# One float32 matmul of 512 columns for two of 256 in the last product of a fused attention and two-MLP kernel

## The chip, the cores and the metric

The kernel runs as one program on one core of one Trainium2 chip. The metric is the time of the whole program on the device in microseconds (us). Engines are named as the profile names them: PE is TensorE (its matmuls), PEld its weight loads, DVE VectorE, ACT ScalarE, POOL GpSimd, SP the engine that issues most transfers.

## The reference, cut to what matters

Causal attention over 4 batches of 8 heads gives `x` of 2304 tokens and 512 features; a first MLP with a normalisation follows, then the second MLP, whose last line the change is about:

```python
def _moe2_ref(x, w_in, w_out):          # x: 2304 x 512, w_in: 512 x 2048, w_out: 2048 x 512
    h = x @ w_in
    relu6 = np.clip(h + 3.0, 0.0, 6.0)
    g = h * relu6 / 6.0
    return (g @ w_out).astype(np.float32)
```

All is float32.

## The kernel before

**Order of the work.** The kernel writes no engine's program by hand. Each piece of work is told to a planner (class `Plan`) with its engine, a duration, what it reads and writes, and buffers or PSUM banks that it takes. `Plan.emit` plays these pieces through with the given durations, lets each engine take the ready piece of lowest rank, and emits the instructions in the order in which they came up; the engines then run their lists strictly in that order. A piece's rank is its running number, changed for some ranges of numbers by the table `MOVED` (line 46), which holds plain running numbers (for instance `(3517, 3518, None, -22)`); the table is the same in both kernels.

**The stages.** Attention comes first, with the first MLP laid between; then the second MLP's first product (`unit`, line 1367), which writes `g` to HBM in transposed form; from 594 us to the end runs the second MLP's second product, `g @ w_out / 6`. It is the stage that the change touches.

**The second product.** The tokens are cut into 9 tiles (`group(bi, t)`, line 1493; 3 `bi` by 3 `t`) of 256 tokens by 512 output columns. Such a tile is computed as a 2 x 2 block product by the scheme with seven products and fifteen sums: `a11, a12, s2, s1, s3, s4, a22` (table `SECOND`, line 1443), each of a 128-token block by a 256-column block of weights, over 8 slices of 128 of the inner dimension. Three accumulators live in PSUM banks, `x`, `y` and `z`: `x` takes `a11`, then `s2`, `s3` and `a22` on top, `y` takes `a12`, `z` takes `s1`, then `s4`.

**High and low.** A float32 factor is split into a rounded high part and the rest, the low part. `form` (line 1525) makes both parts of a token block: ACT casts the high part (line 1533), then DVE, or POOL for two forms of each tile from the third tile on, subtracts to get the low part (line 1537). Four form buffers go round. Before that, DVE makes the sums of the scheme, `n`, `r21`, `r11` and `r12` (`total`, line 1517), each of 128 x 1024. The weights are split beforehand and lie side by side: `W[:, k, 0, :]` is the high and `W[:, k, 1, :]` the low part of 256 columns.

**The matmuls.** `product` (line 1548) issues, for each slice k, high x W high and high x W low (`y = 0`, one piece per two or three slices), then low x W high (`y = 1`), each a matmul of 256 columns into the first 256 columns of the accumulator's bank: 24 matmuls a product, 168 a tile, 1512 in all.

**Reading the banks.** `x` is read in the middle of its accumulation, so that PE may not go on with it until it is read. `keep` (line 1562) copies `x / 6` to SBUF on ACT: `c11` after `a11`, `c12` after `s2`, `c22` after `s3`. `put` (line 1569) makes an output block: on DVE as `bank / 6 + kept` (`y` with `c11`, `z` with `c22` after `s1`, `z` with `c12` after `s4`), on ACT for the last one (`x` after `a22`); SP then stores it. Line 1587 lists these tails.

The planner gives a DVE operation on two SBUF tensors and any POOL operation the same single port (`port`), so that it never plans them side by side.

Of the kernel before, what the change touches and what calls it, by code (L numbers as in the profile page):

```python
# [16 lines left out]
ALU = mybir.AluOpType  # L17
# [187 lines left out]
def act(n, extra=0.09):  # L205
    return extra + 0.00085 * n
# [11 lines left out]
def kernel(ctx, tc, q, k, v, s, w_in, w_out, g_ln, w2_in, w2_out, out):  # L218
    nc = tc.nc
# [4 lines left out]
    P = 128  # L224
# [58 lines left out]
    def bank(key):  # L283
        return banks[plan.bank[key]]
# [147 lines left out]
    NK = KFF2 // 2  # L432
    T = {}
# [107 lines left out]
    plan = Plan()  # L541
# [951 lines left out]
    def group(bi, t):  # L1493


        tag = f"{bi}_{t}"
        nonlocal slots
        mine = slots
        slots = dict(r11=mine["n"], r12=mine["r21"], r21=mine["r11"], r22=mine["r12"], n=mine["r22"])
        key = lambda x: f"{x}_{tag}"  # L1500
        made, done = [], []

        def raw_tile(x):
            i = mine[x]
# [36 lines left out]
        made.append([load("r21", 1, 0), load("r22", 1, 1)] + form("a12", "r12", "DVE"))
        made.append([total("n", "r21", "r22", 1), total("r21", "r11", "r21", 0), total("r11", "n", "r11", 0)] + form("s2", "r11", "DVE"))
        made.append(form("s1", "n", "POOL" if forms_made[0] > 14 else "DVE"))
        made.append(form("s3", "r21", "DVE"))
        made.append([total("r12", "r12", "r11", 0)] + form("s4", "r12", "DVE"))
        made.append(form("a22", "r22", "POOL" if forms_made[0] > 14 else "DVE"))

        def product(x, i, b, first):
            b_key, name = key(f"o{b}"), key(f"f{x}")
            r = []  # L1550
            for y in range(2):
                for q, (k0, k1) in enumerate(PIECES):
                    def mm(y=y, q=q, k0=k0, k1=k1):
                        for k in range(k0, k1):
                            for w in range(2 - y):
                                nc.tensor.matmul(bank(b_key)[:, : 2 * P], lhsT=T[name][:, y, k, :], rhs=T[f"W{i}_{q}"][:, k - k0, w, :],  # L1556
                                                 start=first and k == 0 and y == 0 and w == 0, stop=k == NK - 1 and y == 1, skip_group_check=not first)

                    r.append(lambda mm=mm, y=y, q=q, n=k1 - k0: plan.add("PE", n * (2 - y) * 0.119, mm, reads=[f"{name}/{'hl'[y]}", *(f"W{i}_{q}/{w}" for w in "hl"[: 2 - y])], writes=[b_key], bank=b_key if first and y == q == 0 else None))
            return r  # L1560

        def keep(name, b):
            def go():
                T[key(name)] = pools["mid"].tile([P, W], F32, tag=name, name=key(name), bufs=2)[:, : 2 * P]
                nc.scalar.mul(T[key(name)], bank(key(f"o{b}"))[:, : 2 * P], 1.0 / 6.0)

            return [lambda: plan.add("ACT", act(2 * P), go, reads=[key(f"o{b}")], writes=[key(name)], new=[(name, 2, key(name))])]

        def put(b, h, o, kept):
            ob = key(f"ob{h}{o}")  # L1570

            def go():
                T[ob] = pools["g"].tile([P, W], F32, tag="g", name=ob, bufs=G_BUFS)[:, : 2 * P]
                src = bank(key(f"o{b}"))[:, : 2 * P]
                if kept:
                    nc.vector.scalar_tensor_tensor(out=T[ob], in0=src, scalar=1.0 / 6.0, in1=T[key(kept)], op0=ALU.mult, op1=ALU.add)
                else:
                    nc.scalar.mul(T[ob], src, 1.0 / 6.0)

            def store():  # L1580
                r0 = ((2 * bi + h) * TRIO + t) * P
                nc.sync.dma_start(out=out[r0 : r0 + P, o * 2 * P : (o + 1) * 2 * P], in_=T[ob])

            return [lambda: plan.add(*(("DVE", dve(2 * P)) if kept else ("ACT", act(2 * P))), go, reads=[key(f"o{b}")] + ([key(kept)] if kept else []), writes=[ob], new=[("g", G_BUFS, ob)]),
                    lambda: plan.add("SP", 0.5, store, reads=[ob], writes=[f"out{ob}"], dma=moved(128, 1024))]

        tails = [keep("c11", "x"), put("y", 0, 0, "c11"), keep("c12", "x"), [], keep("c22", "x") + put("z", 1, 1, "c22"), put("z", 0, 1, "c12"), put("x", 1, 0, None)]
        for (x, i, b, first), tail in zip(SECOND, tails):
            done.append(product(x, i, b, first) + tail)
        return made, done  # L1590
# [80 lines left out]
```

## Time and profile before

| | |
|---|---|
| median of 3 runs | 784.19 us (782.44 to 785.3) |
| the profiled execution | 783.54 us, of which its span from first to last instruction is 781.7 us |
| granted TensorE clock, mean | 0.998 of full speed |
| PE busy | 766.9 us, 98% of the span |
| DVE, ACT, POOL busy | 600.4, 476.8, 229.0 us |
| chain of waits that ended last | PE 91%, DVE 3%, ACT 2%, DMA 2%; the second product's matmuls (line 1556) 22% |

The profile is one execution. An engine's busy time counts instructions that overlap only once, and a matmul's listed duration runs from its start to the modelled end of its write, so that a stream of matmuls is read by the distance between starts. The chain of waits is followed back from the last instruction. Below, a "cast" is ACT's high part, a "low" the subtraction that makes the low part.

### The profile page before, as it was taken

To read this page: it belongs to the slowest core of one execution; us is meant where nothing else is said; L and a number is where in the kernel's file an instruction comes from. 1 tells how busy PE (TensorE), PEld (TensorE's weight loads), DVE (VectorE), ACT (ScalarE), POOL (GpSimd) and SP (SyncE) were. 2 spreads that over 40 slices of the span, in tenths; PEclk is the share of its full clock that TensorE was granted. 3 is DMA by queue.
4 is the path that set the end of the run, shared out by engine and by line. 5 is a ranking of instruction groups with operands and counts; after the bars stand their busy time and mean duration, and the time that the engine had idled before them with its cause. 6 is when DMAs were issued, how large, how long until landed. Compare 5 with 4: busy or idle time off the path is not lost.

```text
span 781.7 us, 15872 instructions
## 1 busy us (share of the span) xinstructions
PE 766.9 (98%) x5560; PEld 705.5 (90%) x5560; DVE 600.4 (77%) x1381; ACT 476.8 (61%) x1071; POOL 229.0 (29%) x320
## 2 busy tenths in 40 slices
PE   6999999999999999999999999999999999999998
PEld 5667878988898888888999999999999999999998
DVE  5789988677967787757787897898987877766663
ACT  4889878656767566646474765666675444444332
POOL 3584635344643363252200000000122012222222
PEclk9999999999999999999999999999999999999999
DMA  8867677788577685613533544567599644444440
GB/s 203 207 175 205 167 184 200 200 212 203 142 191 191 185 193 151 182 54 136 157 106 91 197 164 174 184 214 267 157 293 417 199 134 135 137 135 135 136 135 28
DMA packets 157615, 136.33 MB, mean 174 GB/s; under 512 B 67616, under 2 KB 135200, under 8 KB 157536
## 3 DMA queue, kind: packets, MB, share of 16 engines
q1 hardware_dynamic: 153600, 122.07, 55.1%
q10 hardware_dynamic: 2400, 8.54, 3.4%
q0 software_dynamic: 1536, 4.72, 1.5%
q8 instruction: 44, 0.72, 0.4%
q14 instruction: 35, 0.29, 0.1%
HBM read 74.67 MB, written 39.39 MB: 146 GB/s over the span
## 4 chain that ended last, share of the span: by engine, by line
PE 91%; DVE 3%; ACT 2%; DMA 2%; issue 1%; SPq 0%; ACTq 0%; DVEq 0%
PE bank L1556 22%; PE bank L1379 22%; PE bank L1129 13%; PE bank L1039 12%; PE bank L934 6%; PE bank L839 5%; PE bank L907 5%; PE bank L1108 2%; PE bank L688 1%; PE bank L803 1%; DMA s_sb<-in_s_dram 1%; DMA raw_wi<-in_moe_w_in_dram 1%; DMA V0b<-in_v_dram 0%; ACT y L760 0%; DVE y L748 0%
## 5 line engine op out<-in xcount | busy, mean ns | idle before, releaser
L1379 PE MATMUL bank<-xb,ws 128*128 128x384 f32 x1008 | 176.6, 336 | 0.0
L1379 PEld LDWEIGHTS bank<-xb,ws 128*128 128x128 f32 x1008 | 175.3, 188 | 0.0
L1556 PE MATMUL bank<-W,fs 128*128 128x256 f32 x864 | 106.3, 282 | 0.2 <-ACT fs L1533 0.2
L1556 PEld LDWEIGHTS bank<-W,fs 128*128 128x128 f32 x864 | 104.3, 190 | 0.4 <-ACT fs L1533 0.4
L855 POOL TENSOR_SCALAR y<-y,rsum 128x256 f32<-128x256 f32 (+4 forms) x120 | 72.1, 618 | 103.4 <-DVE rsum L851 65.3
L760 ACT ACTIVATE y<-y,nmax 128x384 f32<-128x384 f32 (+4 forms) x140 | 83.4, 598 | 19.9 <-DVE nmax L748 18.0
L748 DVE CUSTOM_DVE_ANT_0 y<-bank,mask 96x288 f32<-96x288 f32 (+4 forms) x168 | 73.5, 466 | 22.1 <-PE bank L839 17.1
L1129 PE MATMUL bank<-zh,w_out_h 128*128 128x256 f32 x288 | 82.3, 286 | 0.0
L1556 PE MATMUL bank<-W,fa 128*128 128x256 f32 x648 | 81.0, 282 | 0.2 <-ACT fa L1533 0.2
L1129 PE MATMUL bank<-zh,w_out_l 128*128 128x256 f32 x288 | 81.0, 281 | 0.0
L1129 PE MATMUL bank<-zl,w_out_h 128*128 128x256 f32 x288 | 80.9, 281 | 0.0
L1556 PEld LDWEIGHTS bank<-W,fa 128*128 128x128 f32 x648 | 78.9, 190 | 0.4 <-ACT fa L1533 0.4
L1413 POOL DMA_DIRECT2D g_d<-g x24 | 13.2, 552 | 184.9 <-DVE g L1408 184.9
L1039 PE MATMUL bank<-w_in_h,xh 128*128 128x512 f32 x144 | 59.6, 414 | 0.1
L839 PE MATMUL bank<-stack 128*96 128x288 f32 (+4 forms) x288 | 58.8, 321 | 0.0
L1039 PE MATMUL bank<-w_in_h,xl 128*128 128x512 f32 x144 | 56.5, 393 | 0.0
L1039 PE MATMUL bank<-w_in_l,xh 128*128 128x512 f32 x144 | 56.5, 392 | 0.0
L1129 PEld LDWEIGHTS bank<-zh,w_out_h 128*128 128x128 f32 x288 | 54.2, 188 | 1.3 <-issue 0.2
L1129 PEld LDWEIGHTS bank<-zh,w_out_l 128*128 128x128 f32 x288 | 54.2, 188 | 0.5
L1392 ACT COPY c<-bank 128x384 f32<-128x384 f32 x72 | 34.2, 478 | 33.3 <-PE bank L1379 31.3
L1129 PEld LDWEIGHTS bank<-zl,w_out_h 128*128 128x128 f32 x288 | 54.3, 188 | 0.0
L907 PE MATMUL bank<-ident,y 128*128 128x128 f32 (+2 forms) x420 | 50.8, 260 | 1.0 <-POOL y L873 0.7
(275 smaller groups left out, 1575.1 us busy)
## 6 DMA issues: line engine op xcount, KB each, us to landing
r<-g_d SPq DMA_DIRECT2D x36, 512.0 KB, 5.8
g_d<-g SPq DMA_DIRECT2D x72, 192.0 KB, 1.9
rawo<-in_moe_w_out_dram SPq DMA_DIRECT2D x16, 512.0 KB, 4.7
rawi<-in_moe_w_in_dram SPq DMA_DIRECT2D x16, 512.0 KB, 5.1
x_d<-x2s SPq DMA_DIRECT2D x36, 128.0 KB, 2.5
xr<-x_d SPq DMA_DIRECT2D x6, 768.0 KB
g_d<-g POOLq DMA_DIRECT2D x24, 192.0 KB, 5.9
W<-wp_d SPq DMA_DIRECT2D x6, 768.0 KB, 10.5
```

The lines of the kernel that those rows point to most:

```text
L748: nc.vector.tensor_tensor_reduce(out=ys[h, t][:n, c0:c1], in0=bank(key)[:n, : c1 - c0], in1=mask[:n, 480 + n - w + c0 : 480 + n - w + c1], ...
L760: nc.scalar.activation(out=y[:n], in_=y[:n], func=AF.Exp, bias=nmax[:n, h, t : t + 1], scale=-1.0, accum_out=sums[:n, h, t : t + 1])
L839: nc.tensor.matmul(bank(key)[:n, : c1 - c0], lhsT=ss[:, 2 - 2 * m, ST[t] : w], rhs=ss[:, 3 - 2 * m, c0:c1], start=(m == 0), stop=(m == 1))
L855: nc.gpsimd.tensor_scalar(ys[h, t][:n], ys[h, t][:n], rsum[:n, h, t : t + 1], 1.0, ALU.mult, ALU.mult)
L907: nc.tensor.transpose(bank(key)[: SZ[jj], c : c + SZ[t]], ys[h, t][: SZ[t], ST[jj] : ST[jj] + SZ[jj]], ident[: SZ[t], : SZ[t]])
L934: nc.tensor.matmul(bank(key)[j * D : (j + 1) * D, lo - c0 : c1 - c0], lhsT=vs[v_key(p, a)][:n, jj, j, :], rhs=pts[pt_key(2 * p + j, a)][:n ...
L1039: nc.tensor.matmul(bank(key), lhsT=xs[i][m // 2][:, kk, :], rhs=(w_in_l if m == 1 else w_in_h)[:, kk, f * 512 : (f + 1) * 512], start=(kk ...
L1108: nc.tensor.transpose(bank(key)[:, m * P : (m + 1) * P], es[i][:, f, m * P : (m + 1) * P], ident)
L1129: nc.tensor.matmul(bank(key)[:, : 2 * P], lhsT=w_out_at(w, kk)[:, m * P : (m + 1) * P], rhs=z[:, kk, :], start=(kk == 0 and i == 0), stop= ...
L1379: nc.tensor.matmul(bank(key)[:, :W], lhsT=T[f"ws{k}"][:, WS_OF[op], a, kc * P : (kc + 1) * P], rhs=x_form(bi, op)[:, b, kc, :], start=(fir ...
L1392: nc.scalar.copy(T[to], bank(key)[:, :W])
L1556: nc.tensor.matmul(bank(b_key)[:, : 2 * P], lhsT=T[name][:, y, k, :], rhs=T[f"W{i}_{q}"][:, k - k0, w, :], start=first and k == 0 and y == ...
```

## The change

High x W high and high x W low of a slice become one matmul of 512 columns over the whole bank: the first 256 columns collect high x W high and, as before, low x W high; the second 256 collect high x W low. A product has 8 matmuls of 512 columns and 8 of 256 in place of 24 of 256. Each of the seven readings of a bank in a tile gets a second one on DVE, which adds the second half divided by 6 to what the first wrote (`rest`). A product that goes on in a bank now waits for both readings, and so does a store.

```diff
                         for k in range(k0, k1):
-                            for w in range(2 - y):
-                                nc.tensor.matmul(bank(b_key)[:, : 2 * P], lhsT=T[name][:, y, k, :], rhs=T[f"W{i}_{q}"][:, k - k0, w, :],
-                                                 start=first and k == 0 and y == 0 and w == 0, stop=k == NK - 1 and y == 1, skip_group_check=not first)
-
-                    r.append(lambda mm=mm, y=y, q=q, n=k1 - k0: plan.add("PE", n * (2 - y) * 0.119, mm, ...
+                            w = T[f"W{i}_{q}"][:, k - k0]
+                            to, by = (bank(b_key), w.rearrange("p w n -> p (w n)")) if y == 0 else (bank(b_key)[:, : 2 * P], w[:, 0, :])
+                            nc.tensor.matmul(to, lhsT=T[name][:, y, k, :], rhs=by, start=first and k == 0 and y == 0, stop=k == NK - 1 and y == 1, skip_group_check=True)
+
+                    r.append(lambda mm=mm, y=y, q=q, n=k1 - k0: plan.add("PE", n * (0.119 if y else 0.23), mm, ...
...
         def keep(name, b):
...
-            return [lambda: plan.add("ACT", act(2 * P), go, reads=[key(f"o{b}")], writes=[key(name)], new=[(name, 2, key(name))])]
+            def rest():
+                nc.vector.scalar_tensor_tensor(out=T[key(name)], in0=bank(key(f"o{b}"))[:, 2 * P :], scalar=1.0 / 6.0, in1=T[key(name)], op0=ALU.mult, op1=ALU.add)
+
+            return [lambda: plan.add("ACT", act(2 * P), go, reads=[key(f"o{b}")], writes=[f"{key(name)}/a"], new=[(name, 2, key(name))]),
+                    lambda: plan.add("DVE", dve(2 * P), rest, reads=[key(f"o{b}"), f"{key(name)}/a"], writes=[f"{key(name)}/b"])]
...
         def put(b, h, o, kept):
...
+            def rest():
+                nc.vector.scalar_tensor_tensor(out=T[ob], in0=bank(key(f"o{b}"))[:, 2 * P :], scalar=1.0 / 6.0, in1=T[ob], op0=ALU.mult, op1=ALU.add)
...
+                    lambda: plan.add("DVE", dve(2 * P), rest, reads=[key(f"o{b}"), f"{ob}/a"], writes=[f"{ob}/b"]),
+                    lambda: plan.add("SP", 0.5, store, reads=[f"{ob}/a", f"{ob}/b"], writes=[f"out{ob}"], dma=moved(128, 1024))]
```

The 63 new pieces shift the running numbers of all later ones, and the new readings and durations go into the plan, so that the order changes too. Three places follow; a name such as `fs1_0_0` is the form of `s1` in tile `0_0`, `W3_0` a third of a weight block, `bank3_98` a PSUM bank, `c12` and `ob` what `keep` and `put` write. In the new kernel `product`'s matmul stands in line 1557, `keep`'s `rest` in line 1568, `put` and its `rest` in 1580 and 1585.

PE in the first tile, before. Here bank 3 is `x`, bank 4 is `y` and bank 0 is `z`; the high matmuls of `a12` stand just ahead, those of `s3` (into bank 3) just behind.

```order
L1556 MATMUL bank0_95<-W3_0_7229,fs1_0_0_7409 128x256 x6
L1556 MATMUL bank0_95<-W3_1_7244,fs1_0_0_7409 128x256 x6
L1556 MATMUL bank0_95<-W3_2_7349,fs1_0_0_7409 128x256 x4
L1556 MATMUL bank3_98<-W6_0_7149,fs2_0_0_7433 128x256 x6
L1556 MATMUL bank3_98<-W6_1_7103,fs2_0_0_7433 128x256 x6
L1556 MATMUL bank3_98<-W6_2_7138,fs2_0_0_7433 128x256 x4
L1556 MATMUL bank3_98<-W6_0_7149,fs2_0_0_7433 128x256 x3
L1556 MATMUL bank3_98<-W6_1_7103,fs2_0_0_7433 128x256 x3
L1556 MATMUL bank3_98<-W6_2_7138,fs2_0_0_7433 128x256 x2
L1556 MATMUL bank4_99<-W1_0_7004,fa12_0_0_7394 128x256 x3
L1556 MATMUL bank4_99<-W1_1_7049,fa12_0_0_7394 128x256 x3
L1556 MATMUL bank4_99<-W1_2_7066,fa12_0_0_7394 128x256 x2
```

PE at the same place now; the high matmuls of `a12` and `s1` stand just ahead, those of `s3` into bank 3 directly behind.

```order
L1557 MATMUL bank0_95<-W3_0_7229,fs1_0_0_7398 128x256 x3
L1557 MATMUL bank0_95<-W3_1_7244,fs1_0_0_7398 128x256 x3
L1557 MATMUL bank0_95<-W3_2_7345,fs1_0_0_7398 128x256 x2
L1557 MATMUL bank4_99<-W1_0_7004,fa12_0_0_7386 128x256 x3
L1557 MATMUL bank4_99<-W1_1_7049,fa12_0_0_7386 128x256 x3
L1557 MATMUL bank4_99<-W1_2_7066,fa12_0_0_7386 128x256 x2
L1557 MATMUL bank3_98<-W6_0_7149,fs2_0_0_7417 128x512 x3
L1557 MATMUL bank3_98<-W6_1_7103,fs2_0_0_7417 128x512 x3
L1557 MATMUL bank3_98<-W6_2_7138,fs2_0_0_7417 128x512 x2
L1557 MATMUL bank3_98<-W6_0_7149,fs2_0_0_7417 128x256 x3
L1557 MATMUL bank3_98<-W6_1_7103,fs2_0_0_7417 128x256 x3
L1557 MATMUL bank3_98<-W6_2_7138,fs2_0_0_7417 128x256 x2
```

`s1`'s low matmuls and `a12`'s have moved ahead of `s2`, and between `s2` and `s3`, both on bank 3, nothing is left.

DVE in the first tile, before:

```order
L1537 TENSOR_TENSOR fs1_0_0_7409<-n_0_0_7396,fs1_0_0_7409 128x1024
L1537 TENSOR_TENSOR fs2_0_0_7433<-r11_0_0_7059,fs2_0_0_7433 128x1024
L1537 TENSOR_TENSOR fa12_0_0_7394<-r12_0_0_7124,fa12_0_0_7394 128x1024
L1537 TENSOR_TENSOR fs3_0_0_7424<-r21_0_0_7158,fs3_0_0_7424 128x1024
L1521 TENSOR_TENSOR r12_0_0_7124<-r12_0_0_7124,r11_0_0_7059 128x1024
L1576 SCALAR_TENSOR_TENSOR ob00_0_0_7503<-bank4_99,c11_0_0_7398 128x256
L1537 TENSOR_TENSOR fa22_0_0_7484<-r22_0_0_7186,fa22_0_0_7484 128x1024
L1537 TENSOR_TENSOR fs4_0_0_7505<-r12_0_0_7124,fs4_0_0_7505 128x1024
L1576 SCALAR_TENSOR_TENSOR ob11_0_0_7542<-bank0_95,c22_0_0_7526 128x256
```

and now:

```order
L1537 TENSOR_TENSOR fs1_0_0_7398<-n_0_0_7388,fs1_0_0_7398 128x1024
L1537 TENSOR_TENSOR fs2_0_0_7417<-r11_0_0_7059,fs2_0_0_7417 128x1024
L1537 TENSOR_TENSOR fa12_0_0_7386<-r12_0_0_7124,fa12_0_0_7386 128x1024
L1568 SCALAR_TENSOR_TENSOR c11_0_0_7390<-bank3_98,c11_0_0_7390 128x256
L1537 TENSOR_TENSOR fs3_0_0_7408<-r21_0_0_7158,fs3_0_0_7408 128x1024
L1580 SCALAR_TENSOR_TENSOR ob00_0_0_7448<-bank4_99,c11_0_0_7390 128x256
L1585 SCALAR_TENSOR_TENSOR ob00_0_0_7448<-bank4_99,ob00_0_0_7448 128x256
L1521 TENSOR_TENSOR r12_0_0_7124<-r12_0_0_7124,r11_0_0_7059 128x1024
L1537 TENSOR_TENSOR fs4_0_0_7466<-r12_0_0_7124,fs4_0_0_7466 128x1024
L1568 SCALAR_TENSOR_TENSOR c12_0_0_7472<-bank3_98,c12_0_0_7472 128x256
```

The reading of `c11`'s second half comes ahead of `s3`'s low; that of `c12` comes behind the sum `r12` and `s4`'s low, the two others of `ob00` ahead of `r12`.

PE in the last tile, before, from the end of `s3` (bank 3 is `x`) to the start of `a22`:

```order
L1556 MATMUL bank3_98<-W4_2_7267,fs3_2_2_9187 128x256 x2
L1556 MATMUL bank0_95<-W3_2_7349,fs1_2_2_9161 128x256 x4
L1556 MATMUL bank0_95<-W3_0_7229,fs1_2_2_9161 128x256 x3
L1556 MATMUL bank0_95<-W3_1_7244,fs1_2_2_9161 128x256 x3
L1556 MATMUL bank0_95<-W3_2_7349,fs1_2_2_9161 128x256 x2
L1556 MATMUL bank3_98<-W5_0_7317,fa22_2_2_9241 128x256 x6
```

and now:

```order
L1557 MATMUL bank3_98<-W4_0_7207,fs3_2_2_8783 128x256 x3
L1557 MATMUL bank3_98<-W4_1_7231,fs3_2_2_8783 128x256 x3
L1557 MATMUL bank3_98<-W4_2_7267,fs3_2_2_8783 128x256 x2
L1557 MATMUL bank3_98<-W5_0_7317,fa22_2_2_8824 128x512 x3
L1557 MATMUL bank3_98<-W5_1_7355,fa22_2_2_8824 128x512 x3
L1557 MATMUL bank0_95<-W2_0_7286,fs4_2_2_8798 128x512 x3
```

`a22` follows `s3` on the same bank directly; the rest of `s1`, which stood between them, has gone ahead of `s3`.

## Rows read from the trace of the kernel before

**Rows 1.** The page's first part: busy us of each engine, share of the span, instructions.

```profile
PE 766.9 (98%) x5560; PEld 705.5 (90%) x5560; DVE 600.4 (77%) x1381; ACT 476.8 (61%) x1071; POOL 229.0 (29%) x320
```

**Rows 2.** Windows: stretch, us; PE, PEld, DVE, ACT, POOL busy; PE clock, DMA share, GB/s.

```profile
604.00:614.00 10.00, 9.84 (x83) 9.64 (x82) 9.03 (x11) 4.55 (x7) 0.54 (x1) 1.00 0.97 338
...
720.00:740.00 20.00, 20.00 (x170) 20.00 (x170) 13.22 (x13) 8.24 (x12) 4.82 (x2) 1.00 0.43 132
```

**Rows 3.** Groups from 590 us on, shapes apart: count, busy us, mean ns | idle before, releaser.

```profile
L1556 PE MATMUL bank<-W,fs 128*128 128x256 f32 x864 | 106.3, 282 | 0.2 <-ACT fs L1533 0.2
```

**Rows 4.** Timelines, ACT and PE, seventh tile: start, duration (us), instruction, [idle before <-releaser].

```profile
719.89 0.38 ACT L1578 ACTIVATE ob<-bank 128x256 f32<-128x256 f32 x1 [5.79 <-PE bank L1556]
...
732.58 1.59 PE L1556 MATMUL bank<-W,fa 128*128 128x256 f32 x12
...
732.78 0.38 ACT L1565 ACTIVATE c<-bank 128x256 f32<-128x256 f32 x1 [1.74 <-PE bank L1556]
...
739.89 0.38 ACT L1578 ACTIVATE ob<-bank 128x256 f32<-128x256 f32 x1 [5.79 <-PE bank L1556]
```

**Rows 5.** Timeline of PE in the first MLP: twelve 512-column matmuls in a row, first and last.

```profile
388.16 0.39 PE L1039 MATMUL bank<-w_in_h,xh 128*128 128x512 f32 x1
...
390.66 0.39 PE L1039 MATMUL bank<-w_in_h,xl 128*128 128x512 f32 x1
```

**Rows 6.** Timeline of DVE in the seventh tile.

```profile
725.85 0.41 DVE L1576 SCALAR_TENSOR_TENSOR ob<-bank,c 128x256 f32<-128x256 f32 x1
726.18 1.21 DVE L1537 TENSOR_TENSOR fs<-r,fs 128x1024 fp32r<-128x1024 f32 x1
...
733.20 0.42 DVE L1576 SCALAR_TENSOR_TENSOR ob<-bank,c 128x256 f32<-128x256 f32 x1 [0.90 <-ACT c L1565]
```

**Rows 7.** Timeline of PE in the first tile.

```profile
600.46 2.18 PE L1556 MATMUL bank<-W,fa 128*128 128x256 f32 x16 [0.19 <-ACT fa L1533]
602.47 2.07 PE L1556 MATMUL bank<-W,fs 128*128 128x256 f32 x16
604.70 3.13 PE L1556 MATMUL bank<-W,fs 128*128 128x256 f32 x24 [0.16 <-ACT fs L1533]
...
612.42 1.58 PE L1556 MATMUL bank<-W,fa 128*128 128x256 f32 x12
```

**Rows 8.** Timeline of DVE in the first tile.

```profile
599.83 1.22 DVE L1521 TENSOR_TENSOR n<-r,r 128x1024 f32<-128x1024 f32 x1
601.08 1.23 DVE L1521 TENSOR_TENSOR r<-r,r 128x1024 f32<-128x1024 f32 x1
...
603.95 1.22 DVE L1537 TENSOR_TENSOR fs<-n,fs 128x1024 fp32r<-128x1024 f32 x1
605.09 1.22 DVE L1537 TENSOR_TENSOR fs<-r,fs 128x1024 fp32r<-128x1024 f32 x1
606.22 1.22 DVE L1537 TENSOR_TENSOR fa<-r,fa 128x1024 fp32r<-128x1024 f32 x1
607.36 1.22 DVE L1537 TENSOR_TENSOR fs<-r,fs 128x1024 fp32r<-128x1024 f32 x1
```

**Rows 9.** Timeline of ACT in the first tile: the cast of `a12`, and that of `s4`.

```profile
599.36 1.05 ACT L1533 CAST fa<-r 128x1024 fp32r<-128x1024 f32 x1 [0.55 <-DMA W<-wp_d]
...
609.80 1.05 ACT L1533 CAST fs<-r 128x1024 fp32r<-128x1024 f32 x1 [0.55 <-DVE r L1521]
```

**Rows 10.** Timeline of POOL in the seventh tile: one low.

```profile
728.47 2.41 POOL L1537 TENSOR_TENSOR fa<-r,fa 128x1024 fp32r<-128x1024 f32 x1 [4.77 <-ACT fa L1533]
```

**Rows 11.** Timelines of POOL and DVE in the fourth tile, where their subtractions meet.

```profile
661.13 1.22 DVE L1521 TENSOR_TENSOR r<-r,r 128x1024 f32<-128x1024 f32 x1
...
661.29 3.33 POOL L1537 TENSOR_TENSOR fs<-n,fs 128x1024 fp32r<-128x1024 f32 x1 [8.98 <-PE bank L1556]
...
662.27 4.58 DVE L1537 TENSOR_TENSOR fs<-r,fs 128x1024 fp32r<-128x1024 f32 x2
```

**Rows 12.** One line's view, DVE on a bank and SBUF: ns min/median/max, first and last start.

```profile
L1115 DVE TENSOR_TENSOR zl<-bank,zh x36: 676/682/693, 82.5 to 414.1; 128x512 fp32r<-128x512 f32 x36
```

More of the change, by code (lines that the diff above doesn't have):

```diff
@@ L1554, in mm @@
                         for k in range(k0, k1):
-                            for w in range(2 - y):
-                                nc.tensor.matmul(bank(b_key)[:, : 2 * P], lhsT=T[name][:, y, k, :], rhs=T[f"W{i}_{q}"][:, k - k0, w, :],
-                                                 start=first and k == 0 and y == 0 and w == 0, stop=k == NK - 1 and y == 1, skip_group_check=not first)
-                    r.append(lambda mm=mm, y=y, q=q, n=k1 - k0: plan.add("PE", n * (2 - y) * 0.119, mm, reads=[f"{name}/{'hl'[y]}", *(f"W{i}_{q}/{w}" for w in "hl"[: 2 - y])], writes=[b_key], bank=b_key if first and y == q == 0 else None))
+                            w = T[f"W{i}_{q}"][:, k - k0]
+                            to, by = (bank(b_key), w.rearrange("p w n -> p (w n)")) if y == 0 else (bank(b_key)[:, : 2 * P], w[:, 0, :])
+                            nc.tensor.matmul(to, lhsT=T[name][:, y, k, :], rhs=by, start=first and k == 0 and y == 0, stop=k == NK - 1 and y == 1, skip_group_check=True)
+                    r.append(lambda mm=mm, y=y, q=q, n=k1 - k0: plan.add("PE", n * (0.119 if y else 0.23), mm, reads=[f"{name}/{'hl'[y]}", *(f"W{i}_{q}/{w}" for w in "hl"[: 2 - y])], writes=[b_key], bank=b_key if first and y == q == 0 else None))
             return r
@@ L1582, in store @@
                 nc.sync.dma_start(out=out[r0 : r0 + P, o * 2 * P : (o + 1) * 2 * P], in_=T[ob])
-            return [lambda: plan.add(*(("DVE", dve(2 * P)) if kept else ("ACT", act(2 * P))), go, reads=[key(f"o{b}")] + ([key(kept)] if kept else []), writes=[ob], new=[("g", G_BUFS, ob)]),
-                    lambda: plan.add("SP", 0.5, store, reads=[ob], writes=[f"out{ob}"], dma=moved(128, 1024))]
+            return [lambda: plan.add(*(("DVE", dve(2 * P)) if kept else ("ACT", act(2 * P))), go, reads=[key(f"o{b}")] + ([f"{key(kept)}/{x}" for x in "ab"] if kept else []), writes=[f"{ob}/a"], new=[("g", G_BUFS, ob)]),
+                    lambda: plan.add("DVE", dve(2 * P), rest, reads=[key(f"o{b}"), f"{ob}/a"], writes=[f"{ob}/b"]),
+                    lambda: plan.add("SP", 0.5, store, reads=[f"{ob}/a", f"{ob}/b"], writes=[f"out{ob}"], dma=moved(128, 1024))]
         tails = [keep("c11", "x"), put("y", 0, 0, "c11"), keep("c12", "x"), [], keep("c22", "x") + put("z", 1, 1, "c22"), put("z", 0, 1, "c12"), put("x", 1, 0, None)]
```

## The prediction, made before the change was run

> **What bounds the kernel now.** I read the page's busy times first: PE has 98% of the span [rows 1]. The windows tell more: in a late tile of the second product PE is busy for 20.00 of 20.00 us at a granted clock of 1.00 and DVE for 13.22; in the first tile DVE has 9.03 of 10.00 us, ACT 4.55 and the DMA engines are full [rows 2]. The groups of instructions show 0.2 us of idle time ahead of 864 of the stage's 1512 matmuls [rows 3]. So after the first tile PE waits for nothing, and what shortens its stream shortens the program until another engine comes late; in the first tile DVE is the one that can. The timelines give the paces from which the sums are made.
>
> **The stream.** A tile repeats after 20.00 us (719.89 to 739.89 [rows 4]); with 168 matmuls that is 119.05 ns for one of 256 columns. Twelve matmuls of 512 columns start over 2.50 us [rows 5], eleven steps of 227.3 ns. Two of 256 take 238.1 ns, so a pair saves 10.8 ns, a product (8 pairs) 0.086 us, the 504 pairs 5.44 us. A product now lasts 8 x 0.2273 + 8 x 0.119 = 2.77 us. This very matmul the trace doesn't show; its bounds are 238.1 ns (nothing saved) and 213.3 ns, 512 columns at 2.4 GHz (24.8 ns saved, 12.5 us in all). I take 227.3, the row of the same width in a stream as dense.
>
> The Trainium skill ("TensorE: Matmul & The Clock Gate", section Back-to-back issue gap) speaks against the change: it gives a gap of columns / 2.4 GHz plus 2.5 ns, hence 109.2 and 215.8 ns, and by these, an estimate, the pair saves 2.6 ns and the stage 1.3 us. Both rows lie some 10 ns above it, so here the trace and not the rule sizes the term.
>
> **The new readings.** There are 63 on DVE. `put`'s like operation takes 0.42 us, and the next instruction starts 0.33 after it (725.85, 726.18 [rows 6]); a second one on the same output waits for the first, which I put at 0.45 from start to start, since dependent sums start 1.25 apart and independent ones 1.14 [rows 8]. Seven in a tile are 2.4 us of DVE, on 13.2 of now 19.4 us: the idle time covers them, and without it each would cost its 0.34. Not covered is what stands between a product and the next one in the same bank. PE's stream of `s3` ends at 732.58, ACT starts 0.20 later [rows 4], DVE 0.42 after ACT's start (733.20 [rows 6]), the reading takes 0.42, and a waiting PE starts 0.05 after what it waits for (cast 599.36 + 1.05, PE 600.46 [rows 7, 9]). PE can go on 1.09 us after its product, 0.45 later than now, and later still when DVE has something ahead of the reading. After a stop it loses 0.11 more (16 matmuls are 1.90, but from 600.46 the next ones start 2.01 later [rows 7]).
>
> **The first tile.** DVE's list up to the low of `a12` is as before, so its times hold: low of `s1` ready at 603.95 + 1.22 = 605.17, of `a12` at 606.22 + 1.22 = 607.44 [rows 8]. PE, by the order shown with the change:
> - high of `a12` from 600.46 (a wait for the cast, which swallows what `a11` saves), 1.82 + 0.11, then high of `s1`: done at 604.21.
> - low of `s1` waits for 605.22: 1.01 idle; done at 606.28.
> - low of `a12` waits for 607.49: 1.21 idle; done at 608.55. Before, `s2` filled this time.
> - `s2` to 611.32.
> - `s3` goes into the bank of `s2`, so `c12` must be read twice. DVE: reading of `c11` at 607.36, low of `s3` 607.70, the two readings of `y` 608.84 and 609.29, `r12` 609.63 to 610.85; ACT casts `s4` (1.05 us; it starts about 0.05 after `r12` [rows 9]) to 611.94; DVE makes its low from 611.97 and only then reads `c12`, 613.11 to 613.53. `s3` starts at 613.58: 2.26 idle.
>
> With 0.11 for each of the three stops, these four products are done at 616.46. Before, it was 612.42, when `a22` starts [rows 7]. So the first tile loses **4.04** net. As bounds for its waits I keep 0 (4.39 better) and, should each low that PE waits for come one subtraction later, 3.4 more.
>
> **The second tile.** DVE starts it with the same list, now a subtraction behind; carried on with the same steps, `c12` is read until 633.90, and PE could have started `s3` at 633.08: 0.87 + 0.11 = **0.98**.
>
> **The other tiles.** From the third on POOL makes two lows. Counted from the end of a tile's `s3`: the second reading of `c22` ends at 1.04, those of `z` at 1.94; PE comes to `s4` at 2.50 (eight high matmuls of the next `a11`, three of `a22`). DVE then runs the low of `a12` (1.86), `n` (3.00), `r21` (4.25), `r11` (5.50), `z` twice (6.64, 7.09), `r12` (7.43), the low of `s2` (8.57), and reads `ob` (9.71) and `c11` (10.05 to 10.47); PE wants that bank at 11.09. Margins of 0.5 and 0.6 us: no wait, by a little.
>
> **The last tile.** `a22` follows `s3` in the same bank with nothing between: 1.09 + 0.11 = **1.20**. The last output has one more reading after ACT's: **0.45**.
>
> **The sum.** The 58 products that follow the first tile's four and `a11` save 58 x 0.0864 = 5.01 us. 4.04 + 0.98 + 1.20 + 0.45 - 5.01 = **+1.7 us**. On the profiled execution's 783.54 that is 785.2, on the median of 784.19 785.9; I say **785.5**. A measurement of this kernel can tell about 0.5% (3.9 us) from no change.
>
> **Rivals.**
> - *The gain arrives.* The first tiles' waits are not real, because the planner would have placed PE's pieces so that they are ready: 1.7 - 4.39 - 0.98 = -3.7 us, 779.8; a little more where the 512 columns come nearer to 213 ns. For it: before, PE lost 0.33 us there in the same game (602.47 + 1.90 = 604.37, start at 604.70 [rows 7]). Against it: DVE's times up to 607.44 are read, not guessed. 0.12.
> - *POOL takes the port first: slower.* Where POOL's low comes while a DVE subtraction runs, the next DVE subtraction waits for the whole of it: POOL asks at 661.29, DVE's sum ends at 662.35, and the following low, begun at 662.27, is through with its successor only 4.58 us later, in place of 2.36 [rows 11]. In each of the seven later tiles the low of `s2` starts at 8.57 and POOL's low of `s1` is ready at 9.11 by the same count (cast of `s2` from 6.76, ACT's last reading, cast of `s1`, some 2.35 us). If DVE is later than POOL by a hair, POOL's 2.41 us [rows 10] stand ahead of the low of `s2` and of the reading of `c11` behind it; that ends at about 13.4 in place of 10.47, and PE stops 2.4 us in seven tiles: 16.8 + 1.7, 802. It decides from 0.54 us of lateness on. Against it: that margin; and the readings themselves, one operand of which is in PSUM, hardly wait (such an operation never took over 693 ns in 36, beside a POOL that was often busy [rows 12]). 0.10. The Trainium skill ("SBUF — State Buffer", section SBUF: two separate sides) says that whichever of the two starts first holds the pair of ports for its whole instruction, on DVE's side for operations with two inputs in SBUF; by it the subtractions would wait here and the readings not. The trace's 4.58 us agrees on the first.
> - *The pair costs what two did.* Writing the whole bank takes 238 ns: the 5.01 fall away, 790.2. The rows of the same width speak against it [rows 5]. 0.04. By the gap that the Trainium skill's page on TensorE, named above, gives, an estimate, 3.8 us of them fall away: 789.0.
> - *The margins of 0.5 are too thin.* Five handovers in a row, each 0.1 to 0.2 longer than read, cost up to 0.5 in seven tiles: 787 to 789. 0.08.
>
> **How the numbers follow.** Forecast 0.66 (no change), gain 0.12 (half of it beyond 0.5%), port 0.10 and pair 0.04 slower, margins 0.08, half of it slower. Faster 0.06, same 0.76, slower 0.18. The range leaves out the port and the lower half of the gain (0.16): 779.8 up to 791, which holds the pair and the margins.
>
> **What would show it.** Right: 512-column matmuls at about 227 ns, 256 still at 119; stops of PE between 604 and 614 us of some 1.0, 1.2 and 2.3 us, behind lows and behind `c12`'s second reading, one of nearly 1 us in the second tile and one of 1.1 near the end; a tile of 19.4 us between. Wrong: a steady tile of 20 us or more, PE waiting for DVE's `c11` in each, or no idle time in the first tile.

## The result, and the profile after

The changed kernel takes 788.25 us (median of 8 executions, 786.46 to 789.08) against 783.89 for the kernel before: ratio 1.0054, 95% interval 1.0038 to 1.0071. The forecast was 785.5 in a range of 779.8 to 791.0, with no measurable change as the likeliest outcome; it came out at the edge of what can be told, half a per cent slower. The second set further down gives 787.13 and 1.0035 (1.0021 to 1.0049).

The profiled execution took 788.91 us, its span 787.1. Its page answers to [rows 1], the windows to [rows 2], the groups to [rows 3]. The page:

```profile
PE 766.2 (97%) x5056; PEld 681.1 (87%) x5056; DVE 621.2 (79%) x1444; ACT 475.4 (60%) x1071; POOL 230.2 (29%) x320
```

PE has 504 matmuls fewer and as much busy time as before; DVE has 63 instructions and 21 us more. The windows (duration, then busy time and instructions of PE, PEld, DVE, ACT and POOL; granted clock of TensorE, DMA share, GB/s):

```profile
604.00:614.00 10.00, 6.19 (x37) 4.93 (x35) 8.78 (x12) 3.55 (x5) 0.54 (x1) 1.00 0.88 308
614.00:624.00 10.00, 9.80 (x43) 8.22 (x44) 5.95 (x8) 2.04 (x3) 0.00 (x0) 0.83 0.36 109
720.00:740.00 20.00, 20.00 (x116) 17.49 (x115) 16.22 (x20) 8.23 (x11) 5.26 (x2) 1.00 0.44 132
```

In the first tile PE fell from 9.84 to 6.19 of 10 us, and over the ten us behind it the granted clock had a mean of 0.83. In a late tile PE is as full as before. What PE waited for in the stage (total us, times, the longest):

```profile
PE bank L1557 <- DVE c L1568: 3.8, 3, 2.1
PE bank L1557 <- DVE fa L1537: 1.1, 1, 1.1
PE bank L1557 <- DVE fs L1537: 0.8, 1, 0.8
```

L1568 is the new second reading of a kept bank: it holds PE three times. The lows of `s1` and `a12` hold it once each. PE's timeline (start, length, instructions; in brackets the idle time ahead and what ended it) shows where; it answers to [rows 4, 7]:

```profile
601.01 2.12 PE L1557 MATMUL bank<-W,fa 128*128 128x512 f32 x8 [0.20 <-ACT fa L1533]
...
605.78 1.22 PE L1557 MATMUL bank<-W,fs 128*128 128x256 f32 x8 [0.81 <-DVE fs L1537]
608.05 1.21 PE L1557 MATMUL bank<-W,fa 128*128 128x256 f32 x8 [1.05 <-DVE fa L1537]
609.10 2.95 PE L1557 MATMUL bank<-W,fs 128*128 128x512 f32 x16
614.20 4.62 PE L1557 MATMUL bank<-W,fs 128*128 128x512 f32 x16 [2.14 <-DVE c L1568]
618.65 2.69 PE L1557 MATMUL bank<-W,fa 128*128 128x512 f32 x11
...
636.27 3.07 PE L1557 MATMUL bank<-W,fs 128*128 128x512 f32 x16 [0.70 <-DVE c L1568]
...
658.78 2.69 PE L1557 MATMUL bank<-W,fa 128*128 128x512 f32 x11
...
678.38 2.69 PE L1557 MATMUL bank<-W,fa 128*128 128x512 f32 x11
...
777.48 1.67 PE L1557 MATMUL bank<-W,fa 128*128 128x512 f32 x6 [0.93 <-DVE c L1568]
```

Three stops in the first tile (0.81, 1.05, 2.14), one in the second (0.70), one in the last (0.93). The rows 614.20 and 636.27 are the same 16 matmuls of `s3`, once 4.62 and once 3.07 us long. Between the stops a tile repeats after 19.60 us (658.78 to 678.38), 0.40 less than before. The chain of waits (start, length, what) gives the way to the 2.14:

```profile
606.86 1.13 DVE fa L1537
608.00 0.34 DVE c L1568
608.33 1.13 DVE fs L1537
609.46 0.35 DVE ob L1580
...
609.83 0.43 DVE ob L1585
610.26 1.14 DVE r L1521
...
611.50 1.06 ACT fs L1533
...
612.58 0.32 DVE fs L1537
...
613.72 0.43 DVE c L1568
...
614.20 15.82 PE bank L1557 x80
```

It is DVE's queue in the order of the prediction: low of `a12`, reading of `c11`, low of `s3`, two of `y`, `r12`, ACT's cast of `s4`, its low, and only then the reading of `c12` on which `s3` waits.

### The profile page after: what moved, and what is told of

Its sections match the earlier page's. It is cut to its first block, busy times and chain, and to the rows that moved or that the text cites. A ratio compares the mean times of both kernels' runs of the same rounds, so it can differ in the third digit from the quotient of the medians.

```text
span 787.1 us, 14967 instructions
## 1 busy us (share of the span) xinstructions
PE 766.2 (97%) x5056; PEld 681.1 (87%) x5056; DVE 621.2 (79%) x1444; ACT 475.4 (60%) x1071; POOL 230.2 (29%) x320
## 5 line engine op out<-in xcount | busy, mean ns | idle before, releaser
L1557 PE MATMUL bank<-W,fs 128*128 128x256 f32 (+1 forms) x576 | 106.4, 341 | 3.6 <-DVE c L1568 2.8
L1557 PEld LDWEIGHTS bank<-W,fs 128*128 128x128 f32 x576 | 91.6, 191 | 18.3 <-DVE c L1568 3.2
L1557 PE MATMUL bank<-W,fa 128*128 128x512 f32 (+1 forms) x432 | 79.4, 338 | 2.2 <-DVE fa L1537 1.1
L1557 PEld LDWEIGHTS bank<-W,fa 128*128 128x128 f32 x432 | 66.4, 189 | 11.0 <-DVE fa L1537 1.3
L1533 ACT CAST fs<-r 128x1024 fp32r<-128x1024 f32 x27 | 28.3, 1050 | 55.3 <-DVE r L1521 42.4
```

Source lines behind the costliest of these rows:

```text
L1557: nc.tensor.matmul(to, lhsT=T[name][:, y, k, :], rhs=by, start=first and k == 0 and y == 0, stop=k == NK - 1 and y == 1, skip_group_check= ...
```

## The experiments

**How the runs are compared.** The executions of one kernel spread over 2 to 6 us, and much of it arises ahead of the changed stage: in these profiles the stage begins between 597.5 and 603.5 us (the latest, of e4, has a granted clock of 0.89 in its first 60 us, the kernel before 0.97). So beside the medians I use the **stage**: from the start of `a12`'s high matmuls (the row at 601.01 above; 600.46 in [rows 7]) to the end of the span, in one profile of each kernel.

| kernel | median us | ratio to before, 95% | stage us |
|---|---|---|---|
| before | 782.94 to 783.89 in four sets | | 181.24 |
| changed | 788.25 | 1.0054 (1.0038 to 1.0071) | 186.09 |
| e1 split again | 789.25 | 1.0068 (1.0047 to 1.0089) | 187.58 |
| e2 no second reading | 781.72 | 0.9976 (0.9964 to 0.9988) | 181.08 |
| e3 table moved | 785.17 | 1.0025 (1.0010 to 1.0040) | 183.86 |
| e4 two tiles narrow | 781.94 | 0.9974 (0.9960 to 0.9988) | 180.32 |
| e5 old order | 781.65 | 0.9980 (0.9967 to 0.9993) | 180.76 |
| e6 reading ahead of `s4` | 785.14 | 1.0035 (1.0021 to 1.0049) | 184.57 |
| e7 three tiles narrow | 780.51 | 0.9966 (0.9953 to 0.9978) | 179.26 |
| e8 old form, new order | 786.88 | 1.0048 (1.0034 to 1.0062) | 184.42 |
| e9 one reading earlier | 784.36 | 1.0005 (0.9992 to 1.0017) | 182.62 |
| e10 first and last narrow | 782.67 | 0.9989 (0.9975 to 1.0002) | 181.55 |
| e11 changed again | 787.13 | 1.0035 (1.0021 to 1.0049) | 186.05 |

The theory is the prediction's, with its sizes corrected by the profile after: the stream saves a little, the stops eat it. Its main rivals: the wide matmul brings nothing here; the table's shifted numbers are the cause; the readings' load on DVE is. Line numbers differ by a few between the kernels.

**e1, the stream alone.** The wide matmul is cut in two, all else stays:

```diff
-to, by = (bank(b_key), w.rearrange("p w n -> p (w n)")) if y == 0 else (bank(b_key)[:, : 2 * P], w[:, 0, :])
-nc.tensor.matmul(to, lhsT=T[name][:, y, k, :], rhs=by, start=first and k == 0 and y == 0, ...)
+for x in range(2 - y):
+    nc.tensor.matmul(bank(b_key)[:, x * 2 * P : (x + 1) * 2 * P], lhsT=T[name][:, y, k, :], rhs=w[:, x, :],
+                     start=first and k == 0 and y == 0 and x == 0, ...)
```

> Each 512-column matmul is cut again into two of 256 into the two halves of the bank; halves, readings, waits and the planned order stay those of the changed kernel's form. Theory (the wide stream saves some 0.057 us a product, the readings and their waits cost the rest): the 63 products take 63 x 0.057 = 3.6 us more than in the changed kernel, the stops of the first, second and last tile stay, so some 3.6 us above the changed kernel, 7 to 8 us above the kernel before (about 791.5). Rival (the wide matmul streams no faster than the pair here, and the whole difference lies elsewhere): as the changed kernel, 4 us above the kernel before. Forecast's size of the saving (0.0864 a product): 5.4 us above the changed kernel, about 793.5.

Measured: 1.0 us above the changed kernel by the medians, with overlapping intervals; 1.5 by the stage. Expected were 3.6. PE's timeline of e1:

```profile
602.98 1.22 PE L1557 MATMUL bank<-W,fs 128*128 128x256 f32 x8 [0.68 <-DVE fs L1537]
605.25 1.22 PE L1557 MATMUL bank<-W,fa 128*128 128x256 f32 x8 [1.05 <-DVE fa L1537]
...
611.39 3.10 PE L1557 MATMUL bank<-W,fs 128*128 128x256 f32 x24 [2.04 <-DVE c L1569]
...
640.47 6.12 PE L1557 MATMUL bank<-W,fa 128*128 128x256 f32 x50
...
660.47 6.12 PE L1557 MATMUL bank<-W,fa 128*128 128x256 f32 x50
```

The stops are there, the tile is back at 20.00 us (640.47 to 660.47). So the wide matmul is worth 0.40 us a tile. The stage says less because `s3` behind the third stop takes 2.95 us here (611.39 to 614.34, the next row) and 4.45 in the changed kernel: that is the clock, below. Without those 1.5 us the stages differ by 3.0, and the stops of e1 are 0.5 us shorter in all (0.68, 2.04 and, in the second tile, 0.42 in place of 0.81, 2.14 and 0.70): together 3.5, where nine tiles of 0.40 make 3.6. The medians alone would not have told it.

**e2, the readings.** All 63 are left out (the edit in short):

```diff
-lambda: plan.add("DVE", dve(2 * P), rest, reads=[key(f"o{b}"), f"{key(name)}/a"], writes=[f"{key(name)}/b"])]
+]
...
-lambda: plan.add("DVE", dve(2 * P), rest, reads=[key(f"o{b}"), f"{ob}/a"], writes=[f"{ob}/b"]),
```

> The second reading of every bank (63 instructions on VectorE) is left out, so the product of the high part with the low part of W is computed and not added. Theory (readings make the waits): no stop of over 0.5 us behind a reading is left, and what remains is the stream's saving, 63 x 0.057 = 3.6 us below the kernel before, about 780.3; the granted clock stays at 1.00 between 614 and 624. Rival (the faster stream alone outruns the low forms of the first tile, and the readings are not to blame): stops of 0.8 and 1.0 us stay in the first tile and the gain is 1 us or less. With the forecast's pitch of 227.3 ns it would be 5.4 us below, 778.5.

Measured: 1.9 us below before instead of the 3.6 expected. No stop of DVE's making is left, but the planner, whose input this changes, made another order, and four waits for ACT came with it; the largest in PE's timeline:

```profile
644.64 8.63 PE L1553 MATMUL bank<-W,fs 128*128 128x512 f32 x48 [1.59 <-ACT fs L1529]
```

With 0.50 and 0.39 in the first tile and 0.24 in the last they are 2.72 us; the stage, 181.08, would be 178.4 without them, 2.9 below before. The forecast's saving of 5.4 doesn't come even without the readings.

**e3, the table.** The order table speaks of instructions by number, and the new readings shift the numbers behind them:

```diff
-(3467, 3487, "DVE", -24), ... (4113, 4128, None, -127), ... (3517, 3518, None, -22), ... (3559, 3564, None, 9), ... (3518, 3541, None, -65),
+(3467, 3488, 'DVE', -24), ... (4172, 4189, None, -139), ... (3520, 3521, None, -23), ... (3566, 3572, None, 10), ... (3521, 3547, None, -68),
```

> The changed kernel with the order table's plain numbers carried along past the new instructions, so that each entry hits the piece that it hit in the kernel before. The order of the first tile's matmuls stays the changed kernel's; in the second tile the pieces of s1 stand between and behind those of s2, in the last tile s1's low pieces stand between s3 and a22. Theory: the stops of 0.70 in the second and 0.93 us in the last tile go or nearly go, those of the first tile and the clock's fall behind them stay: 1.5 to 2 us below the changed kernel, 2.5 to 3 us above the kernel before (about 786.5). Rival (the shifted numbers are the whole cause): at or below the kernel before, 780 to 784.

Measured: 785.17, 3 us below the changed kernel by the medians and 2.2 by the stage. The stops of the second and last tile went, a new one of 0.93 came in the third, and the three of the first stayed (0.82, 1.05, 2.13; the third and the new one):

```profile
612.11 3.08 PE L1553 MATMUL bank<-W,fs 128*128 128x512 f32 x16 [2.13 <-DVE c L1564]
...
652.48 3.08 PE L1553 MATMUL bank<-W,fs 128*128 128x512 f32 x16 [0.93 <-DVE c L1564]
```

In stops the table brings 0.70 us (0.70 and 0.93 less, 0.93 more). The other 1.5 of the stage's 2.2 were not expected: behind the stop of 2.13 us `s3` takes 3.08 and not 4.62, which is the clock, below. So the shifted numbers make up the smaller part of the loss, and the first tile's 4.00 us are not theirs.

**e4, e7, e10, where the new form stands.** The named tiles keep pairs of 256 columns and one reading:

```diff
+NARROW = ("0_0", "0_1")
...
+wide = tag not in NARROW
```

This is e4; in e7 the tiles named are `0_0`, `0_1` and `2_2` (batch and index, the first two and the last), in e10 `0_0` and `2_2`. In e10 the lows of `s1` also stand behind `s2` in the wide tiles.

> The first two of the nine tiles keep the old form (pairs of 256 columns, one reading), the other seven have the new one; table numbers carried along. Theory: no stop in the first two tiles and a full clock there; 7 x 7 products save 49 x 0.057 = 2.8 us, the last tile costs up to 1.0 and the later end 0.45: 1.3 to 2.3 us below the kernel before, about 782.3. Rival (the stops only move to the first tile in the new form): at or above the kernel before, 784 to 787.

> The first two tiles and the last keep the old form (pairs of 256 columns, one reading), the six between have the new one. Theory: no stop of over 0.3 us anywhere behind a second reading, the end as in the kernel before, 6 x 7 products save 42 x 0.057 = 2.4 us: about 781.2 against 783.6, and 0.9 us below the kernel with two tiles in the old form. Rival (the end's stop is not due to the reading): as that kernel, 781.9, or above.

> Only the first and the last tile keep the old form, the seven between have the new one, with s1's low pieces behind s2's. Theory: 49 products save 49 x 0.057 = 2.8 us, stops of 0.2 to 0.5 in all are left in the second and third tile: 780.5 to 781, level with the kernel of three tiles in the old form. Rival (the first tile in the new form meets late low forms wherever it stands): a stop of over 0.8 us in the second tile, 782.

Measured: e4 781.94 and e7 780.51, as the theory has it. In e4 one stop of 0.70 is left ahead of the last tile's `a22`; in e7 this is the only stop of the stage behind a second reading:

```profile
647.82 3.08 PE L1560 MATMUL bank<-W,fs 128*128 128x512 f32 x16 [0.16 <-DVE c L1571]
```

**e7 beats both kernels**, 0.34% below before (interval 0.22 to 0.47%). e10 misses: with the second tile in the new form too, stops come there behind casts and the reading, each smaller than the rival's 0.8 but together (1.18 us) more than the 0.40 that the seventh wide tile saves:

```profile
625.06 2.14 PE L1560 MATMUL bank<-W,fs 128*128 128x512 f32 x8 [0.41 <-ACT fs L1531]
627.52 4.01 PE L1560 MATMUL bank<-W,fs 128*128 128x512 f32 x24 [0.32 <-ACT fs L1531]
631.98 3.07 PE L1560 MATMUL bank<-W,fs 128*128 128x512 f32 x16 [0.45 <-DVE c L1571]
```

**e8, the order alone.** The old form everywhere, but `s1`'s and `a12`'s low pieces ahead of `s2` in the first tile:

```diff
+def behind(x):
+    return [key("oy"), key("oz")] if (tag, x) == ("0_0", "s2") else []
...
+if tag == "0_0":
+    done[2:4] = [], done[3] + done[2]
```

What `behind` returns goes into the reads of the product's pieces. Two entries of the table differ as well; ACT and DVE make `s4`'s parts ahead of `a22`'s, as in the changed kernel.

> The old form everywhere (pairs of 256 columns, one reading), but in the first tile TensorE's order of the changed kernel: s1's and a12's low pieces ahead of s2, s3 directly behind s2. Theory (the order makes the stops, the second reading only a part of one): stops of 0.7 and 1.05 us ahead of the two low products and of 0.8 to 1.3 ahead of s3, which waits for ScalarE's keeping of c12 alone; some 3 us above the kernel before, about 786.6. Rival (without the second readings the order costs nothing): within 0.8 us of the kernel before.

Measured: 786.88; the stage is 3.2 us longer than before with not one matmul or reading changed. PE's timeline:

```profile
602.94 1.22 PE L1559 MATMUL bank<-W,fs 128*128 128x256 f32 x8 [0.67 <-DVE fs L1535]
605.21 1.21 PE L1559 MATMUL bank<-W,fa 128*128 128x256 f32 x8 [1.05 <-DVE fa L1535]
609.77 3.10 PE L1559 MATMUL bank<-W,fs 128*128 128x256 f32 x24 [0.47 <-ACT c L1571]
613.34 0.97 PE L1559 MATMUL bank<-W,fa 128*128 128x256 f32 x6 [0.47 <-ACT c L1571]
```

Two of the changed kernel's three stops are the order's. Of the third (2.14) 0.47 is: behind one reading `s3` starts that much late, behind two and their queue 1.67 later. The last row's 0.47, ahead of `a22`, is this run's own: in the changed kernel matmuls of the next tile's `a11` stand between `s3` and `a22` (in the row 618.65). So some 0.6 of the 3.2 us don't belong to the changed kernel's order.

**e6, what stands ahead of the reading.** In the first tile `s4`'s low waits for `c12`'s second reading; PE's order is untouched:

```diff
-reads=[key(src), f"{name}/h"], writes=[f"{name}/l"]
+reads=[key(src), f"{name}/h"] + [key("c12") + "/b"] * (key(x) == "s4_0_0"), writes=[f"{name}/l"]
...
+if tag == "0_0":
+    made[5:7] = made[5][:-1], made[5][-1:] + made[6]
```

> The changed kernel with TensorE's order untouched; in the first tile alone c12's second reading stands ahead of s4's low form on VectorE. Theory (s3 waits for that reading behind 1.13 us of s4's low form): the reading starts as soon as ScalarE has kept the first half, s3's stop shrinks from 2.14 to 1.3 to 1.4 us, everything behind moves up by 0.8: some 0.8 us below the changed kernel, 787.4 or, where the clock doesn't fall behind the stops, 786. Rival (s3 waits for something else, or s4's late low form stops TensorE in turn): the sum of the first tile's stops stays at 4.0 us.

Measured: 785.14, the stop is 1.28:

```profile
613.74 3.08 PE L1557 MATMUL bank<-W,fs 128*128 128x512 f32 x16 [1.28 <-DVE c L1568]
```

So 0.86 us of the 2.14 was the queue with the low of `s4` in it, as the chain of waits says, and `s3` takes 3.08 again. The stage is 1.5 us shorter than the changed kernel's, less than 0.86 and the 1.5 of `s3` together: in this profile a wait of 0.49 for `s1`'s cast came ahead of the first stops.

**e9, why the order changed.** e3 with one entry more in the table, on `c11`'s second reading in the first tile:

```diff
+(3476, 3477, None, -22),
```

> The changed kernel with the table's numbers carried along and one entry more: c11's second reading in the first tile gets a rank 22 places lower, so that VectorE takes it ahead of s1's low form. With it the planner itself puts the low pieces of s1 and a12 behind s2 instead of ahead of it (a22 now follows s3 directly in the first tile, and two matmuls of s1's low part stand between them in the last). Theory (the late second reading of c11 kept s2's bank taken, so the planner spent the low pieces ahead of s2 and had none left behind it): the stops of 0.82, 1.05 and 2.13 us go, 0.3 for s2's high form and about 1.0 ahead of a22 come, 0.7 in the last tile: 2.5 to 3 us below the kernel with the table carried along, about 782.4. Rival (the new order is due to the shorter stream, the reading has no part in it): stops of 3 us or more stay in the first tile, 785.

Measured: 784.36, 0.8 below e3 and 1.2 by the stage; I had expected 2.5 to 3. The stops ahead of the two lows are gone, which the rival can't explain: `s2` goes into `c11`'s bank, and while that bank was to be read late, the planner filled PE with the lows. But `s3` still waits 1.55 us, and with 0.28 ahead of `s2` and 0.93 ahead of `a22` the first tile's stops are 2.76, near the rival's 3. PE's, ACT's and DVE's timelines in e9:

```profile
610.75 3.08 PE L1554 MATMUL bank<-W,fs 128*128 128x512 f32 x16 [1.55 <-DVE c L1565]
```

```profile
607.73 0.38 ACT L1562 ACTIVATE c<-bank 128x256 f32<-128x256 f32 x1 [3.56 <-PE bank L1554]
```

```profile
608.35 1.22 DVE L1518 TENSOR_TENSOR r<-r,r 128x1024 f32<-128x1024 f32 x1
609.48 0.42 DVE L1577 SCALAR_TENSOR_TENSOR ob<-bank,c 128x256 f32<-128x256 f32 x1
609.94 0.42 DVE L1582 SCALAR_TENSOR_TENSOR ob<-bank,ob 128x256 f32<-128x256 f32 x1
610.28 0.41 DVE L1565 SCALAR_TENSOR_TENSOR c<-bank,c 128x256 f32<-128x256 f32 x1
```

ACT had kept `c12`'s first half by 608.11 (607.73 + 0.38), but the reading (610.28) stands behind `r12` and both readings of `y`. Each urgent reading has to be put forward by itself.

**e5, both readings early and the old order.** That is what e5 does, in the new form everywhere:

```diff
+def behind(x, y):
+    return [key("ox")] if y and (x == "s1" or (tag, x) == ("0_0", "a12")) else []
...
+if tag == "0_0":
+    done[1:3] = done[1][:3], done[2] + done[1][3:]
+if tag in ("0_0", "2_2"):
+    s1, s3 = done[3:5]
+    done[3:5] = s1[:3], s3[:6] + s1[3:] + s3[6:]
...
+(3476, 3477, None, -22), (3498, 3499, None, -100),
```

The two new entries are `c11`'s and `c12`'s second readings. Only the lines that set the order are shown (what `behind` returns goes into the reads of a product's pieces); the table's other entries are carried along to the numbers of this order.

> The new form everywhere, but in the order of the kernel before: in the first tile a12's low pieces stand behind s2's and s1's behind s3's, in the last tile s1's low pieces behind s3's, in the others s1's behind s2's; c11's second reading comes ahead of the low forms on VectorE and c12's ahead of r12. Theory (the stops come from the order that the planner chose for the new form, the readings only lengthen them): in the first tile stops of 0.3 (s2's high form), 0.5 (s3 behind c12's second reading) and at most 0.3 us are left of the 4.0, in the others at most 0.4 each; with 3.3 us of the stream's saving and 0.45 at the end the stage takes 1 us less than in the kernel before, about 782.5 in all. Rival (the second readings load VectorE so far that its queue stays behind, whatever the order): stops of over 2.5 us in the first tile, 785 to 787.

Measured: 781.65 (0.20% below before, 0.07 to 0.33%). The stops of the first tile, in PE's timeline:

```profile
601.79 3.19 PE L1558 MATMUL bank<-W,fs 128*128 128x512 f32 x16 [0.28 <-ACT fs L1531]
606.38 4.02 PE L1558 MATMUL bank<-W,fs 128*128 128x512 f32 x24 [0.25 <-DVE c L1569]
610.91 1.66 PE L1558 MATMUL bank<-W,fa 128*128 128x512 f32 x6 [0.51 <-DVE c L1569]
```

1.04 us in place of 4.00, with every second reading in place; the third tile has one more of 0.20, and the last none. The stage is 0.5 us shorter than before, where 1 was expected. The load of the readings is not the cause; where they stand in DVE's queue is, and which of PE's pieces are left to cover them.

**e11, the clock.** The changed kernel once more, unaltered.

> The changed kernel once more, with its own second profile. Theory (the fall of the granted clock behind the first tile's stops is not part of the change but comes in some executions): stops of 0.8, 1.05, 2.1, 0.7 and 0.9 us as before, and from the start of a12's products to the end 184.5 us with the clock at full or 186.1 with a fall; the median 787.5 to 788.3. Rival (the fall comes with these stops each time): 0.83 between 614 and 624 again, 186.1.

Measured: 787.13, a stage of 186.05, and the clock fell at the same place again. The same window of e11, then of e3:

```profile
614.00:624.00 10.00, 10.00 (x46) 8.37 (x47) 5.87 (x8) 1.58 (x3) 0.00 (x0) 0.85 0.35 103
```

```profile
614.00:624.00 10.00, 10.00 (x61) 8.82 (x60) 7.22 (x11) 2.65 (x5) 0.00 (x0) 1.00 0.24 72
```

The theory named the fall a chance of single executions and the rival a result of the stops. The fall came in both profiles of the changed kernel and in none of e1 and e3, which have nearly the same three stops some 2 us earlier in the span. But it did not come each time: a fall like this takes 0.002 off the mean of the span (0.17 x 10 us of 787), and four of e11's twelve executions have a mean granted clock of 1.000 (784.30, 784.54, 785.49 and 787.08 us). So the rival's "each time" falls; what decides whether the clock falls stays open.

## Why the prediction was right, and where its sizes were off

- **What binds, and where it would stop: right.** Five stops were forecast, in the first tile three (1.01, 1.21 and 2.26), in the second tile one, ahead of the last `a22` one. All five came, behind the instructions named, at 0.81, 1.05, 2.14, 0.70 and 0.93; no steady tile waits. They look a little shorter because the profile counts a stop from the modelled end of the last write and the forecast from the end of the stream: the 16 matmuls of `s2` are listed with 2.95 us, and at this stage's 231 and 119 ns they are 2.80. From start to start the waits fit: the low of `a12` comes 2.27 behind that of `s1` (605.78 to 608.05; forecast 605.22 to 607.49, also 2.27), and `s3` 6.15 behind it (608.05 to 614.20; forecast 6.09).
- **The stream: mis-sized.** "A pair saves 10.8 ns", 5.01 us over 58 products, a tile of 19.4. The tile takes 19.60: 0.40 / 56 pairs is 7.1 ns. With 56 matmuls of 256 columns at 119.05 ns, 12.93 us are left for 56 of 512, 231 ns each; the 227.3 of [rows 5] was right for its stretch and not for this stage. Over 58 products 8.3 tiles x 0.40 = 3.3 us. e1 (0.40 a tile) agrees, and e2 (2.9 in all) comes near.
- **The first tile: right but for the clock.** Four products were to take 16.00 us from 600.46 to 616.46; they took 17.64 (601.01 to 618.65). `s3` alone took 4.45 in place of the 2.92 it takes in e3 (612.11 to 615.03, the row of the next `a11`): 1.53 of the 1.64 are the granted clock, which the sum left at 1.00.
- **Second tile, last tile, end:** 0.98, 1.20 and 0.45 were forecast. Counted from the end of the stream, 0.15 us more than the profile's 0.70 and 0.93, and with the 0.11 that the forecast adds behind a stop, 0.96 and 1.19 came, and 0.46 at the end (from the end of PE's last matmul to the end of the span 3.75, before 3.29).
- **The sum.** +1.7, with 1.7 less saved by the stream and 1.5 lost to the clock, is +4.9; the stages differ by 4.85. The start, 0.55 later in this profile, brings it to the 5.4 by which the profiled executions differ. Both misses went the same way. The range kept its upper part for the pair and the margins, neither of which came about; that it held these 3.2 us too is luck.
- **Rivals.** *The gain arrives* fell with the order of PE's pieces, and e5 shows that part of it could have been had with another order: 1.3 us by the medians, against the 3.7 of the rival. *The pair costs what two did* fell by e1's tile. By the gap of the Trainium skill's page ("TensorE: Matmul & The Clock Gate", section Back-to-back issue gap), given there for an isolated matmul, the widths would take 109.2 and 215.8 ns, an estimate; here they take 119 and 231. The saving of a pair, 7.1 ns, lies between the 2.6 that follow from it and the 10.8 of the rows that I chose.
- *The margins of 0.5 are too thin* did not come: no steady tile waits.
- *POOL takes the port first* did not come in the place that it named: DVE's low of `s2` still started first, 0.61 us ahead of POOL's low of `s1` (forecast 0.54). POOL then held up DVE's next subtraction, the low of `s3`, which the rival did not reckon with and which PE does not wait for. POOL's and DVE's timelines of the changed kernel, seventh tile:

```profile
726.78 2.87 POOL L1537 TENSOR_TENSOR fs<-n,fs 128x1024 fp32r<-128x1024 f32 x1 [10.82 <-ACT fs L1533]
```

```profile
726.17 1.22 DVE L1537 TENSOR_TENSOR fs<-r,fs 128x1024 fp32r<-128x1024 f32 x1
...
727.64 0.41 DVE L1568 SCALAR_TENSOR_TENSOR c<-bank,c 128x256 f32<-128x256 f32 x1
727.97 2.77 DVE L1537 TENSOR_TENSOR fs<-r,fs 128x1024 fp32r<-128x1024 f32 x1
```

Beside POOL's subtraction (726.78 to 729.65) DVE's reading of `c11`'s bank takes its usual 0.41, and its subtraction 2.77 in place of 1.22: it ends at 730.74, 1.09 after POOL's. That is what the Trainium skill's page ("SBUF — State Buffer", section SBUF: two separate sides) says, and here idle time covers it.

## What to carry to other kernels

Where an instruction is merged at the price of one more reading of its result, look for the next writer of that buffer: the reading's place in its engine's queue decides, not its length (here 0.42 us long and up to 2.14 us of stop). A greedy order that met a longer wait here spent its filling work ahead of it and had none left behind it, so look at the order first and then at the operation. And restrict such a change to the part of the loop where the other engines have room: six of nine tiles gave 0.34%, all nine in the changed kernel's order cost 0.5%.

## What the hardware showed that was not expected

- The granted clock had a mean of 0.83 in the 10 us behind the stops of 0.81, 1.05 and 2.14 us, with PE busy for 6.19 of the 10 us ahead of it; there eight matmuls of 512 columns and eight of 256 took 4.45 us in place of 2.92, that is, they ran for the most part at the lower of the two levels, 1.2 in place of 2.4 GHz (the granted clock was 0.58 from 614 to 616 us, 0.57 from 616 to 618 and 1.00 from 618 to 620). To 4.00 us of stops the clock thus added 1.5. Why nearly the same stops left the clock at 1.00 in e1 and e3, and in a part of the changed kernel's own executions, stays open.
- The same width has two paces: 227.3 ns a matmul of 512 columns in [rows 5], 231 in the second product. The 63 readings don't cause it: in e2 PE's timeline repeats a tile after 19.56 us (its `s4` starts at 713.87 and at 733.43), against 19.60 with them. What does was not tried.
